# Two row maxima read by one VectorE instruction, in the attention steps without dense work

## The chip, the core and the metric

The kernel runs on one core of one Trainium2 chip. A core has five engines with queues of their own: TensorE (PE; its weight loads are shown as PEld), VectorE (DVE), ScalarE (ACT), GpSimd (POOL) and SyncE (SP, which issues the transfers here). Matmul results go to banks of 512 float32 values a partition, of which this kernel uses eight, and VectorE and ScalarE read them from there. The metric is device time in microseconds, lower is better.

## The reference

One block of a transformer with adaptive layer norm, over 2048 rows of 512, in float32: attention with 32 heads of 16, then a dense block with mish.

```python
h = _layernorm(x) * (1 + ca) + sa
q, k, v = ...                       # h @ wqkv, 32 heads of 16
scores = jnp.einsum("bhqd,bhkd->bhqk", q, k) * scale
p = _softmax(scores, axis=-1)
x = x + ga * (jnp.einsum("bhqk,bhkd->bhqd", p, v) ... @ wo)
h = _layernorm(x) * (1 + cb) + sb
x = x + gb * (mish(h @ w1 + b1) @ w2)
```

The six vectors `sa, ca, ga, sb, cb, gb` come from `silu(c) @ w_mod`. The softmax needs the largest score of each row (a query of a head) before the exponentials; that largest score is what the change is about.

## The kernel before

The attention is cut into 32 passes (`NIT`): four blocks of 512 queries by eight groups of four heads. A pass has 16 steps, one for each 128 keys' worth of work, so there are T = 512 steps, after 20 steps of lead-in (`PRO`). The order of all work is written out by hand: `step(t)` emits the instructions of step t, each engine takes its own in that order, and the framework adds the waits that the data need. `run_hooks` and `do_specials` put loads, splits and other small work at fixed half-steps.

Products of 64 rows are used throughout. The operands `ka` (keys) and `qa` (queries) hold two heads, one in partitions 0 to 63 and one in 64 to 127, with high and low parts of the numbers as extra rows. A matmul on one half of the rows can run beside one on the other half. A step t has three kinds of them:

- four **scores** (`score`, matmul L519): 128 keys by 512 queries, each followed at once by the exponential on ScalarE (L527) into `pr`. They are all on one half s of the rows; s changes from step to step.
- four **maxima** (`max_tile`, matmul L478): 128 queries by 512 keys (one key block `kb` of four), each followed by a reduction along the row on VectorE (L480), which writes one column of `mx`. They belong to the pass that comes 20 steps later (`tm = t + PRO`). For a query tile and a head the four key blocks give four columns, which `neg_max` (L489) and `max_rows` turn into the row's maximum, and two rows of `qa` later take it off the scores.
- **dense halves** (`mm_half`, L132): the projections, the output projection and the dense block, cut into units and dealt out over the steps by `next_part`. A unit's products run on the half of the rows that the scores leave free.

After these, `pv(t - 2)` issues the value products (L547) of the step two before: four matmuls of 32 columns that accumulate in the bank `acc`.

How the maxima are laid depends on f, the number of dense products of this step. `o = max(0, (8 - f) // 2)` maxima go to the free half (`alone`), the other 4 - o go to the scores' half (`mo`). With f = 0 all four are on the free half, and the last branch of the loop emits score, maximum, score, maximum. f is 0 where no unit is ready; the plan of units leaves that in steps 0, 1, 116 to 135 and 152 to 157. From step 492 on (`tm >= T`) there are no maxima.

Scores and maxima both write to the **ring**, six banks of one tile `ring_t`. `ring(w)` hands out the next bank, or the next two with `w = 2`, for which it first goes on to an even bank. With four scores and four maxima a step takes eight banks out of the six in turn, and the next step begins two further on. A matmul into a bank waits for the reader of what stood there before. After all is emitted, `free_banks` takes away waits between instructions that touch different banks of the ring; an instruction that reads two banks counts for both.

In `step`, `emit` runs a product and keeps what it returns (its exponential or reduction) where the next dense half has to wait for it (`cur["want"]`, `cur["after"]`).

Of the kernel before, what the change touches and what calls it, by code (L numbers as in the profile page):

```python
# [8 lines left out]
F32 = mybir.dt.float32  # L9
F32R = mybir.dt.float32r  # L10
AF = mybir.ActivationFunctionType
ALU = mybir.AluOpType
AX = mybir.AxisListType
# [5 lines left out]
def adaln_block(ctx: ExitStack, tc: tile.TileContext, x, wqkv, wo, w1, b1, w2, c, w_mod, out):  # L19
    nc = tc.nc  # L20
    P = 128
# [6 lines left out]
    TB = 512  # L28
# [4 lines left out]
    T = 16 * NIT  # L33
# [13 lines left out]
    x = x[0]  # L47
    out = out[0]
# [27 lines left out]
    for k in range(DK):  # L76
# [3 lines left out]
                            axis=AX.XY)  # L80
# [66 lines left out]
    def ring(w=1):  # L147
        if w == 2 and ring_at[0] % 2:
            ring_at[0] += 1
        b = ring_at[0] % NRING  # L150
        ring_at[0] += w
        return ring_t[:, b, :] if w == 1 else ring_t[:, b:b + 2, :]
# [37 lines left out]
    NR = 5  # L190
    kq = ctx.enter_context(tc.tile_pool(name="kq", bufs=1))
    ka = [kq.tile([P, S], F32R, name=f"ka{i}") for i in range(2)]
    qa = [kq.tile([P, TB], F32R, name=f"qa{i}") for i in range(NR)]
# [116 lines left out]
    with ExitStack() as es:  # L310
# [28 lines left out]
        e = lp.tile([P, DK], F32, name="sil_e")  # L339
# [46 lines left out]
        pr, pm = [], ring()[:, :2 * DK].rearrange("p (i k) -> p i k", k=DK)  # L386
        for i in range(2):
            pr.append(ring())
            for k in range(DK):
                nc.tensor.matmul(pr[i][32 * k:32 * k + 32, :], sil[:, k:k + 1].to_broadcast([P, 32]), wma[i][:, k, :],  # L390
                                 start=True, stop=True)
# [67 lines left out]
    ap = ctx.enter_context(tc.tile_pool(name="ap", bufs=1, reuse_waits="tile"))  # L459
# [8 lines left out]
    mxs = {}  # L468

    def max_tile(n, j, s, qs, kb):  # L470

        if n not in mxs:
            mxs[n] = ap.tile([P, 2, 8, 4], F32, tag="mx", name="mx", bufs=2)

        def product():
            kt, qt = ka[(2 * n + j) % NR], qa[(2 * n + j) % NR]
            pm = ring()
            nc.tensor.matmul(pm, qt[64 * s:64 * s + 64, qs * P:(qs + 1) * P], kt[64 * s:64 * s + 64, kb * TB:(kb + 1) * TB],  # L478
                             start=True, stop=True)
            return nc.vector.tensor_reduce(out=mxs[n][:, s, 4 * j + qs, kb:kb + 1], in_=pm, op=ALU.max, axis=AX.X)  # L480

        return product

    def neg_max(n):

        mx = mxs.pop(n)
        mm = ap.tile([P, 4, 2, 4], F32, tag="mm", name="mm", bufs=2)
        twice = bass.AP(tensor=mx.tensor, offset=mx.offset, ap=[list(mx.ap)[0], [16, 4], [0, 2], [4, 4], [1, 4]])
        nc.vector.tensor_reduce(out=mm, in_=twice, op=ALU.max, axis=AX.X)  # L489
        ats.setdefault(16 * n + 16 - PRO, []).append(lambda: max_rows(n, mm))  # L490
# [48 lines left out]
    def pv(t):  # L539
        if not 0 <= t < T:  # L540
            return
        n, kc = divmod(t, 16)
        if kc == 0:
            accs[n] = bank("acc")
        for h in range(4):
            o = (kc * 4 + h) * VW
            nc.tensor.matmul(accs[n][32 * h:32 * h + 32, :], vgs[n][:, o:o + 32], pts.pop((t, h)),  # L547
                             start=(kc == 0), stop=(kc == 15))
        if kc == 15:
            evac(n)  # L550
# [551 lines left out]
    cur = {"left": [], "fin": None, "part": [], "first": True}  # L1102
# [27 lines left out]
    def whole_units(h, credit):  # L1130

        while credit > 0:
            if not cur["left"]:
                if not units or h < units[0][0]():
                    return
                cur["tag"] = "acc" if cur.get("tag") == "ms" else "ms"
                cur["h"] = h
                cur["fin"] = units.pop(0)[1](cur["tag"])
                cur["left"] = list(pe_queue)
                pe_queue.clear()  # L1140
            m = cur["left"].pop(0)
            cur["first"] = False
            mm_go(m)
            credit -= m[0].shape[-1] / TB
            if not cur["left"]:
                at(h + 1, lambda fin=cur["fin"]: fin(h + 1))
                cur["fin"] = None

    def maxima(n, u, s, others):

        j, qs = divmod(u, 4)
        return ([max_tile(n, j, s, qs, kb) for kb in range(4 - others)],
                [max_tile(n, j, 1 - s, qs, kb) for kb in range(4 - others, 4)])

    def step(t):
        second = t % 2
        n, u = t // 16, t % 16 // 2
        tm = t + PRO
        run_hooks(2 * t)
        if t < 0:  # L1160

            for i in range(2):
                if tm < 16:
                    kb, jq = divmod(2 * tm + i, 8)
                else:
                    jq, kb = tm % 16 // 2, 2 * second + i
                for s in range(2):
                    max_tile(tm // 16, jq // 4, s, jq % 4, kb)()
            if second and tm % 16 == 15:
                neg_max(tm // 16)  # L1170
            run_hooks(2 * t + 1)
            for f in ats.pop(t, []):
                f()
            whole_units(2 * t + 1, CREDIT)
            do_specials(2 * t + 1)
            return
        s = 0 if second else 1
        own, others = ([score(n, j, v, 2 * u + i) for i in range(2) for j in range(2)] for v in (s, 1 - s))
        if not second and 1 < t < T:
            next_part(2 * t)  # L1180
        part = list(cur["part"])
        f = len(part)
        if t >= T:
            if t == T:
                cur["tag"] = "acc"
            run_hooks(2 * t + 1)
            pv(t - 2)
            whole_units(2 * t + 1, 8)
            do_specials(2 * t + 1)
            return  # L1190
        swap, held = False, None
        if tm < T:
            o = max(0, (8 - f) // 2)
            mo, alone = maxima(tm // 16, tm % 16 // 2, s, o)

            mine = [x for p in zip(mo, own) for x in p] + own[len(mo):]
            kinds = [k for p in zip("m" * len(mo), "s" * len(mo)) for k in p] + ["s"] * (len(own) - len(mo))
            swap = 2 <= f <= len(mine) and kinds[f - 1] == "s" and kinds[f - 2] == "m"
            if swap:
                mine[f - 2:f] = mine[f - 1], mine[f - 2]  # L1200
        else:
            o = max(0, (4 - f) // 2)
            mine = own[o:] if second else own[:4 - o]
            alone = others[4 - o:] if second else others[:o]

            m = len(mine)
            if f > m:
                mine = [mine[(i * m) // f] if (i + 1) * m // f > i * m // f else None for i in range(f)]
        beside = part + alone

        def emit(product):
            e = product()
            if cur.pop("want", None):
                cur["after"] = e

        ends = second and f and not cur["left"]
        for i in range(max(len(mine), len(beside))):
            if i == len(mine) // 2:
                run_hooks(2 * t + 1)
            if i < f:  # L1220
                last = i + 1 == f
                if i < len(mine) and mine[i] and not last:
                    if swap and ends and i + 2 == f:
                        held = mine[i](True)
                    else:
                        emit(mine[i])
                for m in beside[i]:
                    mm_half(m, second, cur["first"], bool(ends and last and m is beside[i][-1]),
                            cur.pop("after", None))
                    cur["first"] = False  # L1230
                if last:
                    if ends:
                        cur["fin"](2 * t + 2)
                        cur["fin"] = None
                    if held:
                        held()
                    cur["want"] = True
                    if i < len(mine) and mine[i]:
                        emit(mine[i])
            else:  # L1240
                for x in (*mine[i:i + 1], *beside[i:i + 1]):
                    emit(x)
        if tm < T and tm % 16 == 15:
            neg_max(tm // 16)
        do_specials(2 * t + 1, False)
        pv(t - 2)
        if t in ats:
            for f in ats.pop(t):
                f()
        else:  # L1250
            do_specials(2 * t + 1, True)

    def do_specials(h, behind=None):
        if specials and behind in (None, specials[0][2]) and h >= specials[0][0]():
            fin = specials.pop(0)[1]()
            pe_run()
            at(h + 1, lambda: fin(h + 1))
# [94 lines left out]
    def run_hooks(h):  # L1352
        while h in hooks:
            for f in hooks.pop(h):
                f()
# [37 lines left out]
```

## Time and profile before

| | us |
|---|---|
| median of 3 runs | 1679.77 |
| lowest and highest run | 1678.62, 1679.84 |
| the profiled execution | 1677.17 |
| its span in the profile | 1675.4 |
| VectorE busy in it | 1425.7 |
| ScalarE busy in it | 1336.4 |
| GpSimd busy in it | 910.9 |

The profile is one execution. Its page gives busy time by engine and groups of instructions by line; other views group instructions by line in a stretch of time, or list them in order of time. A group's line shows engine, operation, what is written from what, shape and count, then busy time and the mean length of one, then how long the engine sat idle before them and which instruction ended that. Matmul ends are modelled, so a busy TensorE isn't TensorE at its peak. A wait is put to the releaser that came last.

### The profile page before, as it was taken

What the parts mean: (1) busy time and instruction counts of PE and PEld (TensorE: products, weight loads), DVE (VectorE), ACT (ScalarE), POOL (GpSimd) and SP (SyncE); (2) the same over time, 40 slices, a digit from 0 to 9 for tenths busy, and PEclk for the clock granted to TensorE, in tenths of its full rate; (3) what the DMA queues carried; (4) which work ended last, traced back from release to release, by engine and by line L of the source; (5) the groups of instructions that cost most, each with busy time, mean ns of one, the idle gap of its engine ahead of it and who ended that gap; (6) DMA issues with size and microseconds to landing.
All of it is one profiled execution on the core that took longest, in us unless ns stands there. A gap on an engine that the chain in (4) does not pass through costs nothing.

```text
span 1675.4 us, 33101 instructions
## 1 busy us (share of the span) xinstructions
PE 1649.3 (98%) x12316; PEld 921.4 (55%) x12316; DVE 1425.7 (85%) x2327; ACT 1336.4 (80%) x2625; POOL 910.9 (54%) x938
## 2 busy tenths in 40 slices
PE   7999999999999999999999999999999999999999
PEld 5755665555435455555555555555555555554687
DVE  6888898888998988888888888888888888882577
ACT  6257778787779899888889898888889889889364
POOL 5155215465434398854535498654535597645532
PEclk9999999999999999999999999999999999999999
DMA  7677456777684443435343644334442645332362
GB/s 253 186 224 226 110 168 198 236 229 226 201 254 113 111 107 86 119 78 160 86 126 75 200 105 97 102 108 121 121 102 72 178 104 134 87 116 84 126 228 73
DMA packets 113992, 240.03 MB, mean 143 GB/s; under 512 B 24048, under 2 KB 49648, under 8 KB 107784
## 3 DMA queue, kind: packets, MB, share of 16 engines
q1 hardware_dynamic: 113832, 237.92, 50.4%
q8 instruction: 97, 1.59, 0.4%
q14 instruction: 63, 0.52, 0.1%
HBM read 179.95 MB, written 51.44 MB: 138 GB/s over the span
## 4 chain that ended last, share of the span: by engine, by line
PE 83%; POOL 5%; DMA 4%; ACT 4%; DVE 2%; SPq 1%; issue 1%; ACTq 0%; DVEq 0%; POOLq 0%
PE bk L547 27%; PE ring L478 22%; PE ring L519 21%; PE bk L132 6%; PE ring L126 2%; ACT pr L527 2%; PE ring L1088 2%; DMA ka<-kscr 1%; PE bk L126 1%; DVE mx L480 1%; DMA wr<-in_A_wqkv 1%; DMA xt<-in_A_x 1%; POOL rr L781 1%; POOL ee L779 1%; POOL hb L786 1%
## 5 line engine op out<-in xcount | busy, mean ns | idle before, releaser
L480 DVE TENSOR_REDUCE mx<-ring 128x1 f32<-128x512 f32 x2048 | 1278.8, 684 | 159.5 <-PE bk L132 96.0
L527 ACT ACTIVATE pr<-ring 128x512 f32<-128x512 f32 x2048 | 1087.8, 603 | 197.9 <-PE bk L132 159.8
L478 PE MATMUL ring<-ka,qa 64*128 64x512 f32 x2048 | 773.9, 425 | 1.5 <-ACT pr L527 0.8
L519 PE MATMUL ring<-qa,ka 64*128 64x512 f32 x2048 | 719.3, 395 | 6.6 <-ACT pr L527 4.9
L478 PEld LDWEIGHTS ring<-ka,qa 64*128 64x128 f32 x2048 | 365.9, 184 | 396.0 <-DVE mx L480 351.6
L547 PE MATMUL bk<-pr,vg 128*32 128x512 f32 x4096 | 545.1, 604 | 0.0
L519 PEld LDWEIGHTS ring<-qa,ka 64*128 64x128 f32 x2048 | 374.3, 184 | 113.8 <-ACT pr L527 37.7
L132 PE MATMUL bk<-h,w 64*128 64x512 f32 x1008 | 279.9, 409 | 0.0
L132 PE MATMUL bk<-w,a_h 64*128 64x512 f32 x576 | 194.7, 417 | 1.2 <-ACT pr L527 0.6
L132 PEld LDWEIGHTS bk<-h,w 64*128 64x128 f32 x1008 | 171.5, 184 | 2.9 <-ACT yd L906 0.9
L547 PEld LDWEIGHTS bk<-pr,vg 128*32 128x32 f32 x4096 | 80.9, 108 | 127.2 <-issue 120.0
L132 PE MATMUL bk<-w,a_l 64*128 64x512 f32 x288 | 113.9, 396 | 0.0
L749 POOL TENSOR_SCALAR ee<-hb 128x512 f32<-128x512 f32 x42 | 62.5, 1488 | 93.6 <-ACT hb L743 85.1
L132 PEld LDWEIGHTS bk<-w,a_h 64*128 64x128 f32 x576 | 95.4, 185 | 5.3 <-ACT pr L527 1.8
L779 POOL TENSOR_TENSOR ee<-ee,rr 128x512 f32<-128x512 f32 x42 | 54.0, 1285 | 75.5 <-ACT rr L770 75.3
L132 PE MATMUL bk<-w,o_hl 64*128 64x512 f32 x288 | 79.5, 408 | 0.0
L98 POOL TENSOR_TENSOR a_l<-hb,a_h 128x512 fp32r<-128x512 f32 x53 | 71.7, 1354 | 4.4
L907 POOL TENSOR_TENSOR y<-yd,y 128x512 f32<-128x512 f32 x40 | 51.5, 1287 | 28.2 <-ACT yd L906 28.0
L502 POOL TENSOR_TENSOR mt<-mt,mh 32x128 fp32r<-32x128 f32 x32 | 14.4, 450 | 87.9 <-ACT mh L501 87.9
L132 PE MATMUL bk<-h_h,wl 64*128 64x512 f32 x168 | 56.8, 418 | 0.0
L787 POOL TENSOR_TENSOR hb<-hb,rr 128x512 f32<-128x512 f32 x42 | 54.5, 1298 | 3.3
L764 POOL TENSOR_TENSOR ee<-ee,rr 128x512 f32<-128x512 f32 x42 | 54.0, 1287 | 3.5
(211 smaller groups left out, 1847.9 us busy)
## 6 DMA issues: line engine op xcount, KB each, us to landing
ka<-kscr SPq DMA_DIRECT2D x124, 384.0 KB
w<-w2scr SPq DMA_DIRECT2D x56, 512.0 KB
w<-w1scr SPq DMA_DIRECT2D x46, 512.0 KB
vg<-vscr SPq DMA_DIRECT2D x32, 552.0 KB
qa<-qscr SPq DMA_DIRECT2D x124, 100.0 KB
kscr<-qh SPq DMA_DIRECT2D x16, 512.0 KB
qscr<-qh SPq DMA_DIRECT2D x32, 256.0 KB
w1scr<-hl SPq DMA_DIRECT2D x14, 512.0 KB
```

What stands on the lines that cost most here:

```text
L98: (nc.gpsimd if eng == "p" else nc.vector).tensor_sub(lo, src, hi.bitcast(F32))
L132: i = nc.tensor.matmul(acc, l[64 * g:64 * g + 64], r[64 * g:64 * g + 64], start=start, stop=stop)
L478: nc.tensor.matmul(pm, qt[64 * s:64 * s + 64, qs * P:(qs + 1) * P], kt[64 * s:64 * s + 64, kb * TB:(kb + 1) * TB], start=True, stop=True)
L480: return nc.vector.tensor_reduce(out=mxs[n][:, s, 4 * j + qs, kb:kb + 1], in_=pm, op=ALU.max, axis=AX.X)
L519: nc.tensor.matmul(p_, kt[64 * s:64 * s + 64, kc * P:(kc + 1) * P], qt[64 * s:64 * s + 64, :], start=True, stop=True)
L527: e = nc.scalar.activation(pr, p_, AF.Exp, scale=SCALE)
L547: nc.tensor.matmul(accs[n][32 * h:32 * h + 32, :], vgs[n][:, o:o + 32], pts.pop((t, h)), start=(kc == 0), stop=(kc == 15))
L749: nc.gpsimd.tensor_scalar_min(buf("ee", 2), b["hb"], HCAP)
L764: nc.gpsimd.tensor_mul(ee, ee, rr)
L779: nc.gpsimd.tensor_mul(ee, ee, rr)
L787: nc.gpsimd.tensor_mul(hb, hb, rr)
L907: nc.gpsimd.tensor_add(y[i], yd, y[i])
```

## The change

In a step with f = 0 and maxima to make, the four maxima come from the new `max_pairs`. The product for an even key block takes two neighbouring banks of the ring and writes the first; it has no reduction and returns nothing. The product for the next key block writes the second bank, and one reduction reads both banks (128 x 2 x 512) and writes two neighbouring columns of `mx`. Such a step emits maximum, score, maximum, score, in place of score first. Since a product may now return nothing, `emit` asks for that. Steps with dense halves, and those from 492 on, are as before.

```diff
+    def max_pairs(n, u, s):
+
+        if n not in mxs:
+            mxs[n] = ap.tile([P, 2, 8, 4], F32, tag="mx", name="mx", bufs=2)
+        j, qs = divmod(u, 4)
+        made = []
+
+        def product(kb):
+            kt, qt = ka[(2 * n + j) % NR], qa[(2 * n + j) % NR]
+            if kb % 2 == 0:
+                made.append(ring(2))
+            pm = made[-1]
+            nc.tensor.matmul(pm[:, kb % 2, :], qt[64 * s:64 * s + 64, qs * P:(qs + 1) * P],
+                             kt[64 * s:64 * s + 64, kb * TB:(kb + 1) * TB], start=True, stop=True)
+            if kb % 2:
+                return nc.vector.tensor_reduce(out=mxs[n][:, s, 4 * j + qs, kb - 1:kb + 1], in_=pm, op=ALU.max, axis=AX.X)
+
+        return [lambda kb=kb: product(kb) for kb in range(4)]
...
-            mo, alone = maxima(tm // 16, tm % 16 // 2, s, o)
+            mo, alone = maxima(tm // 16, tm % 16 // 2, s, o) if f else ([], max_pairs(tm // 16, tm % 16 // 2, 1 - s))
...
-            if cur.pop("want", None):
+            if e is not None and cur.pop("want", None):
                 cur["after"] = e
...
-                for x in (*mine[i:i + 1], *beside[i:i + 1]):
+                for x in (*mine[i:i + 1], *beside[i:i + 1]) if f or tm >= T else (beside[i], mine[i]):
                     emit(x)
```

## The prediction

> **What bounds the kernel now.** I read the page first, for the engine shares and for the group of reductions that the change joins.
>
> ```profile
> span 1675.4 us, 33101 instructions
> PE 1649.3 (98%) x12316; PEld 921.4 (55%) x12316; DVE 1425.7 (85%) x2327; ACT 1336.4 (80%) x2625; POOL 910.9 (54%) x938
> ...
> L480 DVE TENSOR_REDUCE mx<-ring 128x1 f32<-128x512 f32 x2048 | 1278.8, 684 | 159.5 <-PE bk L132 96.0
> ```
>
> TensorE is nearly always occupied, so time added to its queue anywhere shows in the end. The change touches only steps whose dense part is empty. To find them I asked for busy time by stretch, of the dense halves' line L132 alone; the columns are the stretch, its length, busy time and count on PE and on PEld, granted clock, DMA share and GB/s.
>
> ```profile
> 102.50:106.50 4.00, 0.00 (x0) 0.00 (x0) 1.00 0.65 188
> ...
> 438.79:493.91 55.12, 0.00 (x0) 0.00 (x0) 1.00 0.80 228
> 493.91:539.95 46.04, 26.49 (x96) 16.43 (x96) 1.00 0.47 132
> 539.95:557.04 17.09, 0.00 (x0) 0.00 (x0) 1.00 0.47 165
> ```
>
> The same view for the reductions L480, busy time and count on DVE:
>
> ```profile
> 438.79:493.91 55.12, 49.56 (x80) 1.00 0.80 228
> 539.95:557.04 17.09, 14.78 (x24) 1.00 0.47 165
> ```
>
> Four reductions make a step, so these stretches are 20 and 6 steps without dense halves (steps 116 to 135 and 152 to 157 by the plan of units); the first row is steps 0 and 1. That is 28 of 512 steps, some 76 us: 17.09 + 55.12 + 4.00. The timeline shows one of them (start, duration, engine, line; weight loads mostly left out).
>
> ```profile
> 449.73 1.07 PE L547 MATMUL bk<-pr,vg 128*32 128x512 f32 x8
> 450.72 0.49 PE L519 MATMUL ring<-qa,ka 64*128 64x512 f32 x1
> ...
> 450.73 0.49 PE L478 MATMUL ring<-ka,qa 64*128 64x512 f32 x1
> ...
> 451.06 0.39 PE L519 MATMUL ring<-qa,ka 64*128 64x512 f32 x1
> ...
> 451.06 0.39 PE L478 MATMUL ring<-ka,qa 64*128 64x512 f32 x1
> ...
> 451.25 1.57 ACT L527 ACTIVATE pr<-ring 128x512 f32<-128x512 f32 x3 [0.66 <-PE ring L478]
> 451.29 1.88 DVE L480 TENSOR_REDUCE mx<-ring 128x1 f32<-128x512 f32 x3 [0.24 <-PE ring L478]
> 451.29 0.39 PE L519 MATMUL ring<-qa,ka 64*128 64x512 f32 x1
> 451.29 0.39 PE L478 MATMUL ring<-ka,qa 64*128 64x512 f32 x1
> ...
> 451.90 0.18 PEld L519 LDWEIGHTS ring<-qa,ka 64*128 64x128 f32 x1 [0.62 <-ACT pr L527]
> ...
> 452.03 0.50 PE L478 MATMUL ring<-ka,qa 64*128 64x512 f32 x1
> ...
> 452.46 0.64 PE L547 MATMUL bk<-pr,vg 128*32 128x512 f32 x4
> ```
>
> The step repeats every 2.73 us (449.73 to 452.46). Its pairs of score (L519) and maximum (L478), one on each half of the array's rows, start at 450.72, 451.06 and 451.29. The fourth stops for 0.61 us. The ring has six banks and a pair takes two, so the fourth pair takes the banks of the first: its score waits for the first exponential (from 451.25) and its maximum for the first reduction (451.29 + 0.684 = 451.97, matmul at 452.03, so 0.06 from the end of a read to the release). So the limit here is a delay round the ring, not VectorE's load: value products, first pair, its readers, fourth pair. Waits in the 20 steps say the same: waiter, releaser, us, times, longest.
>
> ```profile
> PEld ring L519 <- ACT pr L527: 27.8, 39, 1.1
> ```
>
> **The change part by part.** Two single reductions become one over two banks. For its length, from the groups of VectorE by form (busy, mean ns):
>
> ```profile
> L562 DVE COPY ot<-bk 128x256 f32<-128x256 f32 x32 | 13.6, 424 | 6.9 <-PE bk L547 6.9
> ...
> L906 DVE COPY yd<-bk 128x512 f32<-128x512 f32 x1 | 0.7, 690 | 8.8 <-PE ring L519 8.8
> ```
>
> 256 more elements from the matmul banks cost 690 - 424 = 266 ns, so 512 more cost 0.53 us and the joint read takes 0.684 + 0.53 = 1.22 us. No row shows a reduction of 1024. Bounds: 1.07 if there were no fixed part (1024 elements at 1.04 ns), 1.37 for two whole reads. I take 1.22, the slope of the nearest rows. What joining saves in VectorE's pace is less than 1.37 - 1.22, for single reads overlap already:
>
> ```profile
> 103.41 7.26 DVE L480 TENSOR_REDUCE mx<-ring 128x1 f32<-128x512 f32 x12 [0.85 <-PE ring L478]
> ```
>
> Twelve end to end give (7.26 - 0.684) / 11 = 0.60 each, so a pair goes from 1.20 to about 1.13 and a step saves 0.13 us of VectorE. The Trainium skill (VectorE: DVE Perf Modes, section "The DRAIN you can't avoid") has the next operation start only when the pipe of the one before is empty; by that rule a step would save 2 x 0.15 = 0.30 us. The trace's 0.60 us spacing against 0.684 us of one speaks against it.
>
> What moves is the release of banks. Call a step's banks r0 to r5 in the order of taking. Now the first pair of maxima takes r0 and r1, its scores r2 and r3, the second pair of maxima r4 and r5, and the last two scores come round to r0 and r1. The third score so waits for the joint read of the **same step**, which can start only when the second maximum is made. And since a step takes eight banks of six, the next step begins two further on: its first two scores land on this step's r4 and r5 and wait for the second joint read. The order max, score, max, score is one queue, so the fourth maximum stands behind the third score, and the next step's second maximum behind its first score. Both joint reads are in a loop with TensorE.
>
> The lags come from rows. Behind a released matmul, the other half's follows in 0.03 us; the last matmul of a step starts 0.32 us ahead of the value products when it isn't held:
>
> ```profile
> 105.95 0.50 PE L478 MATMUL ring<-ka,qa 64*128 64x512 f32 x1
> ...
> 105.98 0.50 PE L519 MATMUL ring<-qa,ka 64*128 64x512 f32 x1
> ```
>
> ```profile
> 1525.28 1.06 PE L547 MATMUL bk<-pr,vg 128*32 128x512 f32 x8
> ...
> 1527.08 0.39 PE L519 MATMUL ring<-qa,ka 64*128 64x512 f32 x1
> 1527.40 0.64 PE L547 MATMUL bk<-pr,vg 128*32 128x512 f32 x4
> ```
>
> A read starts 0.56 us after a first matmul (450.73 to 451.29, 0.07 after its end), and by the same 0.07 it starts 0.39 + 0.07 = 0.46 after one in a run. Let the third score start at 0. The fourth starts at 0.34 (450.72 to 451.06), the value products at 0.66, and the next step's first pair 0.99 later at 1.65. The fourth maximum started at 0.03, so the second joint read runs from 0.59 to 1.81, and the next step's first score goes at 1.87. Its second maximum can start at 1.99 (0.34 behind the first), its read at 2.45 to 2.55, ends at 3.67 to 3.77, and the third score goes at 3.73 to 3.83. I take **3.80** (the held score breaks the run, so the longer lag is nearer). A step loses 3.80 - 2.73 = 1.07 us; 26 steps lose **27.8 us**.
>
> Steps 0 and 1 have no value products ahead of them, and are paced by the twelve reductions above.
>
> ```profile
> 102.87 0.50 PE L478 MATMUL ring<-ka,qa 64*128 64x512 f32 x1
> ...
> 109.60 1.06 PE L547 MATMUL bk<-pr,vg 128*32 128x512 f32 x8
> ```
>
> With joint reads the four run one after the other: second maximum at 103.21, read 103.67 to 104.89, held score 104.95, next read 105.55 to 106.77, then 107.43 to 108.65 and 109.31 to 110.53. Step 2's third slot needs a bank of that last read: 110.59, then 0.34 and four times 0.23 to its last slot at 111.85, and value products at 112.2 in place of 109.60: **+2.5 us**, between +1.5 (step 3 starts with VectorE less behind) and +4.
>
> No DMA, hook or queue of SP or POOL moves against the steps: eight banks are taken per step as before, so later bank numbers stand too. The exponentials of the last two scores come 1 us later, but their readers come two steps on. The sum is 30.3 us. The profiled run took 1677.17 us (span 1675.4, 1.8 around it), so 1707.5 by its own time; the median shown, 1679.77, is 2.6 above that run, so **1710**.
>
> **The rivals.** *Not slower: VectorE's saving counts.* It decides if the third score doesn't wait longer than the fourth pair does now, that is, if r0 is free by 1.18 us after the first pair (450.72 to 451.90). The joint read ends at 0.34 + 0.46 + 1.22 = 2.02, 0.8 too late; it would need the first bank to be given back half way through the read. Nothing in the trace shows such a release; every bank wait ends after its reader. If it were so, the step would go toward VectorE's 2 x 1.13 + 0.24 = 2.5 us, 0.23 under now: 28 steps, -6 us, 1673. The floor is the 2.12 us of a step without maxima (1525.28 to 1527.40).
>
> *Given back.* The added time would let late transfers land and shorten later waits. But the 16 dense steps between the stretches already take 46.04 / 16 = 2.88 us on a busy TensorE, so there is nothing near 27 us to recover: 1680.
>
> *The clock falls.* TensorE would pause some 1.4 us in every step. It has paused about as long here, with no loss of clock (columns: PE, PEld, DVE, ACT, POOL busy, then the granted clock):
>
> ```profile
> 102.84 0.18 PEld L519 LDWEIGHTS ring<-qa,ka 64*128 64x128 f32 x1 [1.38 <-DVE mx L480]
> ```
> ```profile
> 100.50:104.50 4.00, 2.82 (x14) 1.65 (x13) 3.15 (x6) 2.33 (x5) 3.73 (x5) 1.00 0.72 255
> ```
>
> At half the clock TensorE's part of the loop (0.34 + 0.32 + 0.99 + 0.34 + 0.46 = 2.45 us) would come twice: 26 x 2.45 = 64 us more, 1774. The Trainium skill (TensorE: Matmul & The Clock Gate, "A second HAM failure mode: psum-queue depth-cycling") tells of a kernel in which cycling through banks made TensorE pause so often that its clock went to and fro. By that page the time would go towards this rival's; the clock of 1.00 above speaks against it, for single pauses.
>
> *Does the change do what it says?* A joint read split into two would show 2048 reductions of 512 still; the access is plain, two neighbouring banks, so I count it within the range's upper bound.
>
> **How the numbers follow.** Forecast, slower by some 30 us: 0.90. Not slower by the early release: 0.05 (0.04 faster, 0.01 same). Given back: 0.02. The clock: 0.03. With a read of 1.07 us a step takes 3.65 and the sum is 26 x 0.92 + 2 = 26 us, 1706; with 1.37, both reads count (0.59 + 1.37 + 0.06 + 0.03, then 0.56 + 1.37 + 0.06 = 4.04) and the sum is 26 x 1.31 + 3 = 37, 1717. With 1 to 2 us for the lags, 1704 to 1718; cases outside hold about 0.15. 0.2% (3.4 us) is about what a measurement of this kernel can tell from no change. Faster 0.04, same 0.03, slower 0.93.
>
> **What would show it.** 56 reductions over 128x1024, near 1.22 us; the 20-step stretch at about 76 us in place of 55.12, with a wait of scores (L519) for the reduction in place of that for the exponential, twice a step; dense steps unchanged. A step still at 2.73 or less would refute the ring's turn; a step much beyond 4.04 would point to the clock or to a wait that I don't see.

## The result and the profile after

| | before | changed |
|---|---|---|
| median, us | 1679.78 | 1706.78 |
| lowest and highest of 4 runs | 1678.62, 1679.84 | 1706.01, 1708.73 |
| profiled execution, us | 1677.17 | 1708.73 |
| its span | 1675.4 | 1707.0 |

The changed kernel is slower by a factor of 1.0161, 95% interval 1.0149 to 1.0173, or 27.0 us between the medians. The forecast was 1710, with 1704 to 1718 as its range.

From the page of the changed kernel, the span and the engines' busy time:

```profile
span 1707.0 us, 33044 instructions
PE 1657.6 (97%) x12316; PEld 924.2 (54%) x12316; DVE 1425.8 (84%) x2271; ACT 1338.9 (78%) x2625; POOL 909.6 (53%) x938
```

VectorE has 56 instructions fewer and is busy for as long as before (1425.8 against 1425.7): joining the reads gave it nothing back. Its groups by form show why:

```profile
L480 DVE TENSOR_REDUCE mx<-ring 128x1 f32<-128x512 f32 x1936 | 1209.8, 685 | 152.5 <-PE bk L132 93.6 <-PE ring L478 56.7
L499 DVE TENSOR_REDUCE mx<-ring 128x2 f32<-128x1024 f32 x56 | 68.6, 1225 | 36.3 <-PE ring L496 31.0 <-PE ring L538 5.3
```

A joint read is 1.225 us long. But single reads overlap, and joint ones here never do: each has idle time of VectorE ahead of it, 36.3 us in all. (In this kernel the lines are 19 further down: scores are L538, the exponential L546, the value products L566; the maxima of the changed steps are L496, their joint read L499.)

Busy time by stretch, of the joint reads alone. The columns are the stretch, its length, busy time and count on DVE, granted clock, DMA share and GB/s. The stretches run from the first value products of one step to those of another: the 20 steps, the 16 dense ones behind them, the 6 steps. (The joint read counted in the dense stretch is the last of the 20 steps; it runs over.)

```profile
445.48:519.74 74.26, 47.86 (x40) 1.00 0.64 189
519.74:565.87 46.13, 1.13 (x1) 1.00 0.37 99
565.87:588.97 23.10, 13.49 (x12) 1.00 0.35 121
```

The 20 steps take 74.26 us in place of 55.12, the six 23.10 in place of 17.09, and the dense ones between them 46.13, as before (46.04). That is 19.1 + 6.0 = 25.1 us. One step, from the timeline:

```profile
455.93 0.50 PE L538 MATMUL ring<-qa,ka 64*128 64x512 f32 x1 [1.08 <-DVE mx L499]
...
455.93 0.49 PE L496 MATMUL ring<-ka,qa 64*128 64x512 f32 x1
...
456.27 0.39 PE L538 MATMUL ring<-qa,ka 64*128 64x512 f32 x1
...
456.50 1.22 DVE L499 TENSOR_REDUCE mx<-ring 128x2 f32<-128x1024 f32 x1 [0.62 <-PE ring L538]
...
456.59 1.06 PE L566 MATMUL bk<-pr,vg 128*32 128x512 f32 x8
...
457.59 0.50 PE L496 MATMUL ring<-ka,qa 64*128 64x512 f32 x1
...
457.78 0.50 PE L538 MATMUL ring<-qa,ka 64*128 64x512 f32 x1
...
457.93 0.39 PE L496 MATMUL ring<-ka,qa 64*128 64x512 f32 x1
...
458.35 1.23 DVE L499 TENSOR_REDUCE mx<-ring 128x2 f32<-128x1024 f32 x1 [0.47 <-PE ring L496]
...
459.63 0.49 PE L538 MATMUL ring<-qa,ka 64*128 64x512 f32 x1 [1.08 <-DVE mx L499]
```

Read it from the third score at 455.93: fourth maximum beside it, joint read from 456.50, next step's first score released at 457.78, second maximum at 457.93, joint read from 458.35 to 459.58, third score at 459.63. The loop is 3.70 us. Before, the fourth score waited for an exponential; the waits of the 20 steps now name the joint read, once on the weight load and once on the matmul:

```profile
PEld ring L538 <- DVE mx L499: 29.8, 20, 1.6
...
PE ring L538 <- DVE mx L499: 21.4, 20, 1.1
```

The two spans differ by 31.6 us: 25.1 in the 26 steps, 3.4 from the first score to the first value products (102.87 to 109.60 before, 105.97 to 116.11 now), and 3.1 ahead of that, where the kernels are alike. Kernels that leave the beginning as it was also had the first score there: at 106.19, 105.23 and 105.58 us in the traces of e4, e5 and e8 below. So the 3.1 us belong to the single execution.

### The profile page after: what moved, and what is told of

Same layout as the page of the kernel before. It is cut to its first block, busy times and chain, and to the rows that moved or that the text cites. A ratio compares the mean times of both kernels' runs of the same rounds, so it can differ in the third digit from the quotient of the medians.

```text
span 1707.0 us, 33044 instructions
## 1 busy us (share of the span) xinstructions
PE 1657.6 (97%) x12316; PEld 924.2 (54%) x12316; DVE 1425.8 (84%) x2271; ACT 1338.9 (78%) x2625; POOL 909.6 (53%) x938
## 4 chain that ended last, share of the span: by engine, by line
PE 86%; DVE 4%; POOL 4%; DMA 3%; ACT 2%; issue 1%; SPq 1%; ACTq 0%; POOLq 0%; DVEq 0%
PE bk L566 27%; PE ring L478 21%; PE ring L538 21%; PE bk L132 7%; PE ring L126 3%; DVE mx L499 2%; PE bk L126 2%; PE ring L1107 2%; DMA qscr<-ql 1%; ACT pr L546 1%; PE ring L496 1%; DMA wr<-in_A_wqkv 1%; DMA ka<-kscr 1%; DMA wma<-in_w_mod 1%; POOL hb L806 0%
## 5 line engine op out<-in xcount | busy, mean ns | idle before, releaser
L480 DVE TENSOR_REDUCE mx<-ring 128x1 f32<-128x512 f32 x1936 | 1209.8, 685 | 152.5 <-PE bk L132 93.6
L546 ACT ACTIVATE pr<-ring 128x512 f32<-128x512 f32 x2048 | 1090.0, 603 | 224.1 <-PE bk L132 147.0
L538 PE MATMUL ring<-qa,ka 64*128 64x512 f32 x2048 | 718.6, 395 | 30.6 <-DVE mx L499 29.7
L478 PE MATMUL ring<-ka,qa 64*128 64x512 f32 x1936 | 732.3, 424 | 0.9 <-ACT pr L546 0.3
L478 PEld LDWEIGHTS ring<-ka,qa 64*128 64x128 f32 x1936 | 347.6, 184 | 395.1 <-DVE mx L480 350.9
L566 PE MATMUL bk<-pr,vg 128*32 128x512 f32 x4096 | 545.1, 604 | 0.0
L538 PEld LDWEIGHTS ring<-qa,ka 64*128 64x128 f32 x2048 | 373.0, 185 | 116.0 <-DVE mx L499 42.1
L566 PEld LDWEIGHTS bk<-pr,vg 128*32 128x32 f32 x4096 | 80.9, 108 | 130.4 <-issue 123.2
L499 DVE TENSOR_REDUCE mx<-ring 128x2 f32<-128x1024 f32 x56 | 68.6, 1225 | 36.3 <-PE ring L496 31.0
L798 POOL TENSOR_TENSOR ee<-ee,rr 128x512 f32<-128x512 f32 x42 | 53.9, 1284 | 75.5 <-ACT rr L789 75.3
```

Source lines behind the costliest of these rows:

```text
L538: nc.tensor.matmul(p_, kt[64 * s:64 * s + 64, kc * P:(kc + 1) * P], qt[64 * s:64 * s + 64, :], start=True, stop=True)
L546: e = nc.scalar.activation(pr, p_, AF.Exp, scale=SCALE)
L798: nc.gpsimd.tensor_mul(ee, ee, rr)
```

## Experiments

Theory A: the time comes from when banks are given back. A joint read holds two banks until its end, and in a ring of six, of which a step takes eight, the third score and the next step's first score stand behind such reads. Rival B: a read over two banks is itself slow. Rival C: the order, maximum ahead of score, does it. Times of the 20 and 6 steps below are taken, as above, between starts of value products in each trace.

**e1: banks and order of the change, single reads.**

```diff
-            if kb % 2:
-                return nc.vector.tensor_reduce(out=mxs[n][:, s, 4 * j + qs, kb - 1:kb + 1], in_=pm, ...)
+            return nc.vector.tensor_reduce(out=mxs[n][:, s, 4 * j + qs, kb:kb + 1], in_=pm[:, kb % 2, :], ...)
```

> Banks and order of the changed kernel, but each bank read by a reduction of its own. Theory A (release of banks: the third score waits for the reader of its own step's first maximum): the score waits only to the end of the first single read, 0.57 + 0.68 + 0.06 = 1.31 us after the first pair, and the fourth to the end of the second, about 1.91; value products at 2.34, next pair at 3.33, so a step of about 3.3 us between 2.73 and 3.70, and some 1694 to 1697 us in all. Rival B (the read over two banks is what costs, the turn of the banks is harmless): 2.73 us a step, 1680. Rival C (the length of the read doesn't matter at all, only the order): 3.70 us a step, 1707.

Measured: 1694.72 us, ratio 1.0083 (1.0068 to 1.0099). A step from the timeline (L537 score, L496 maximum, L498 single read, L565 value products):

```profile
458.03 1.07 PE L565 MATMUL bk<-pr,vg 128*32 128x512 f32 x8
...
459.02 0.49 PE L496 MATMUL ring<-ka,qa 64*128 64x512 f32 x1
...
460.30 0.50 PE L537 MATMUL ring<-qa,ka 64*128 64x512 f32 x1 [0.31 <-DVE mx L498]
...
460.90 0.50 PE L537 MATMUL ring<-qa,ka 64*128 64x512 f32 x1
...
461.33 1.06 PE L565 MATMUL bk<-pr,vg 128*32 128x512 f32 x8
```

The third score goes 1.28 us after the first pair (459.02 to 460.30; 1.31 was said), the fourth at 1.88, and a step takes 3.30 us. So the change's 0.97 us a step has two parts: 0.57 because both last scores follow the step's own first two maxima in turn, and 0.40 that come with the joint reads, which give both banks back only at their end. B and C both fall as whole explanations. That the 0.40 are the late release, and not a read that is slow in itself, only e3 and e8 below show.

**e2: the order alone.** The kernel before, with the change's last hunk (maximum, then score) and nothing else.

> The kernel before with maximum ahead of score in the steps without dense halves, nothing else. Theory A: no wait changes its place, since a pair still takes two banks and comes round to the same kinds three pairs later; 2.73 us a step, 1680 (1678 to 1682). Rival C (the order by itself holds the score back): over 3 us a step, 1688 or more.

Measured: 1679.28 us, ratio 0.9993 (0.9984 to 1.0003); the 20 steps take 55.46 us. The order costs nothing. One part of the expectation was wrong: a wait does change its place. The maximum is now first in the queue, so the wait in the ring is now put to the reduction and no longer to the exponential (the weight loads of the 20 steps, 40 times), and a step in the middle takes 2.70 us.

```profile
PEld ring L478 <- DVE mx L480: 29.4, 40, 0.8
```

**e3: joint reads, but no product behind one of its own step.** Two banks for the scores, two for each pair of maxima; the order is score, max, score, max, max, max, score, score.

```diff
+        if not f and tm < T:
+            ring_at[0] += -ring_at[0] % NRING
...
+            two = ring(2)
+            for i, x in enumerate((mine[0], beside[0], mine[1], *beside[1:], mine[2], mine[3])):
...
+                if x in mine:
+                    x(p_=two[:, mine.index(x) % 2, :])
+                else:
+                    x()
```

> Joint reads kept, but the scores of such a step have two banks of their own and each pair of maxima two; order score, max, score, max, max, max, score, score. Theory A: no product waits for a joint read of its own step; the third score waits for the first exponential (1.18 us after the first pair), the fourth for the second (1.70), value products at about 2.1, so 3.05 to 3.1 us a step, 9 us over the kernel before: 1687 to 1691. Rival B (joint reads of 1.22 us are themselves too slow or collide with the matmuls): a step stays near 3.7 us, 1704 to 1707.

Measured: 1693.45 us, ratio 1.0073 (1.0058 to 1.0088).

```profile
456.09 1.07 PE L566 MATMUL bk<-pr,vg 128*32 128x512 f32 x8
...
457.08 0.50 PE L538 MATMUL ring<-qa,ka 64*128 64x512 f32 x1
...
457.88 2.36 DVE L499 TENSOR_REDUCE mx<-ring 128x2 f32<-128x1024 f32 x2 [0.74 <-PE ring L496]
458.26 0.18 PEld L538 LDWEIGHTS ring<-qa,ka 64*128 64x128 f32 x1 [0.42 <-ACT pr L546]
...
458.75 0.18 PEld L538 LDWEIGHTS ring<-qa,ka 64*128 64x128 f32 x1 [0.30 <-ACT pr L546]
...
459.18 0.16 PEld L566 LDWEIGHTS bk<-pr,vg 128*32 128x32 f32 x8 [0.24 <-issue]
```

A step takes 3.09 us, as A says: the same 1.22 us reads, now two end to end in 2.36 us, and the last scores wait for exponentials. The whole is 2.5 us over the expected range. The trace's six steps took 21.27 us where 6 x 3.09 is 18.5: small transposes take banks of the ring there, and the fixed layout runs into them; and from the first score to the first value products it took 8.89 us against 6.73 before, most of it at a clock of 0.50 (granted from 105.5 to 112.3 us).

**e4: the kernel before, value products ahead of the fourth pair.**

```diff
+                if i == 3 and not f and tm < T:
+                    pv(t - 2)
                 for x in (*mine[i:i + 1], *beside[i:i + 1]):
...
+        if f or tm >= T:
+            pv(t - 2)
```

> The kernel before, with the value products of these steps issued between the third and the fourth pair. If the step of 2.73 us is a delay round the ring (the fourth pair waits for the readers of the first while TensorE stands still), the value products fill that wait and the step falls to VectorE's pace of four reductions at 0.60, 2.40 us: some 8 us less, 1670 to 1673. Rival (VectorE or ScalarE sets 2.73 us already): 1679 to 1681.

Measured: 1681.39 us, ratio 1.0000 (0.9990 to 1.0009). The expectation fails:

```profile
453.71 1.07 PE L547 MATMUL bk<-pr,vg 128*32 128x512 f32 x8
...
454.70 0.50 PE L519 MATMUL ring<-qa,ka 64*128 64x512 f32 x1
...
455.89 0.50 PE L519 MATMUL ring<-qa,ka 64*128 64x512 f32 x1 [0.21 <-ACT pr L527]
...
456.44 1.06 PE L547 MATMUL bk<-pr,vg 128*32 128x512 f32 x8
```

The step is still 2.73 us. The fourth pair goes at once at 454.70, but between two groups of value products there are four pairs wherever one puts them, and the ring holds three. The fourth behind the value products now is the next step's third, and it starts 1.19 us behind the first (1.18 before). I had taken away one wait and not looked which pair would stand there next.

**e5: joint reads from step 116 on only** (`if f or t < 2` in both conditions).

> The changed kernel, but with single reductions in steps 0 and 1 as before. In the trace of the changed kernel the way from the first score to the first value products took 10.14 us against 6.73, and the granted clock fell to 0.50 in it. Theory A with the clock: that goes, so about 3.4 us under the changed kernel, 1703 to 1704, and the clock stays at 1.00 throughout. Rival (the clock fell by chance, or the price sits in the 26 steps alone): 1706 to 1707.

Measured: 1706.43 us, ratio 1.0154 (1.0139 to 1.0169). The first score to the first value products took 6.93 us in its trace, and the 20 steps 74.24. But the whole was expected at 1703 to 1704, and the clock at 1.00 throughout; both failed. The clock fell there too (0.62 granted between 108 and 112 us), so its fall isn't bound to joint reads. Against the changed kernel's 1706.78 the whole can't tell 3.4 us from nothing, which e9 does.

**e6: the change, value products ahead of the third score.**

```diff
+                    if i == 2 and not f and tm < T and x is mine[i]:
+                        pv(t - 2)
                     emit(x)
...
+        if f or tm >= T:
+            pv(t - 2)
```

> The changed kernel with the value products issued ahead of the third score, into the time in which it waits. Theory A with two loops: the loop through the second joint read (score at 0, fourth maximum, read from 0.57 to 1.79, next step's first score 1.85, second maximum, read from 2.4, third score about 3.65 to 3.70) holds the step alone, so nothing is won: 3.65 to 3.70 us a step, 1705 to 1708. Rival (only the third score's wait counts and TensorE's 0.99 us of value products stands in the way behind it): about 2.7 us a step, 1681.

Measured: 1708.62 us, ratio 1.0172 (1.0158 to 1.0185), 0.6 us over the expected range.

```profile
463.70 1.07 PE L566 MATMUL bk<-pr,vg 128*32 128x512 f32 x8
...
466.73 0.50 PE L538 MATMUL ring<-qa,ka 64*128 64x512 f32 x1 [0.88 <-DVE mx L499]
...
467.39 1.06 PE L566 MATMUL bk<-pr,vg 128*32 128x512 f32 x8
```

3.69 us: nothing won. The value products now lie in the third score's wait, and the next step's first score still waits for the second joint read (second row). The loop through these holds the step without the value products.

**e7 and e10: the kernel before with a seventh bank.** The bank `ms`, which the dense units leave free in the 26 steps, takes the fourth maximum, ahead of the fourth score.

```diff
+                if i == 3 and not f and 2 <= t < T - PRO:
+                    beside[3](bank("ms"))
+                    emit(mine[3])
+                    ring_at[0] += 1
+                    continue
```

> The kernel before, but in the 26 steps without dense halves the fourth maximum goes, ahead of the fourth score, to the bank that the dense units leave free there. Theory A (the step is a delay round the banks): the fourth score still waits for the first exponential, 1.18 us after the first pair, but the fourth maximum no longer for the first reduction (1.31), so 0.13 us a step less: 2.60 us, 3 us less in all, 1677 to 1679 beside a kernel before at 1680 to 1681. Rival (value products or VectorE's pace): 2.73 us and no difference.

> The kernel of the seventh bank once more, for one question: in its trace step 128 stood 3.27 us for the rows of the maxima that SyncE copies into qa, and the clock fell to 0.50 behind it. If that wait comes from the shorter steps, it is there again and the 20 steps take about 58 us; if it was a late transfer of that one execution, the 20 steps take about 52.5 us (20 x 2.61 and 0.3 for the rest) at a clock of 1.00.

Measured: e7 1679.59 us, ratio 1.0003 (0.9994 to 1.0012), which can't be told from the kernel before and lies just above the expected 1677 to 1679; e10, the same kernel, 1679.03 in its one run. In e10's trace the step is what was said, 2.60 us:

```profile
457.72 1.06 PE L547 MATMUL bk<-pr,vg 128*32 128x512 f32 x8
...
459.52 0.39 PE L478 MATMUL bk<-ka,qa 64*128 64x512 f32 x1
...
459.90 0.50 PE L519 MATMUL ring<-qa,ka 64*128 64x512 f32 x1
...
460.32 1.07 PE L547 MATMUL bk<-pr,vg 128*32 128x512 f32 x8
```

Its 20 steps took 52.96 us at a clock of 1.00 (55.12 before), the six 16.76 (17.09), the dense ones between 46.49 (46.04): some 2 us in all, under what was expected and within the noise. e7's own trace had 58.61 us for the 20 steps, for one wait, which e10 doesn't have; so it isn't the shorter steps that make it:

```profile
479.05 0.47 PE L519 MATMUL ring<-qa,ka 64*128 64x512 f32 x1 [3.27 <-DMA qa<-mt]
```

**e8: joint reads on seven banks.** Steps 0 and 1 as before; in the 26 steps scores go to two banks of the ring and to `ms`, and only the fourth score waits, for the first exponential.

```diff
+            two = ring(2)
+            to = [two[:, 0, :], two[:, 1, :], bank("ms"), two[:, 0, :]]
+            for i in range(4):
...
+                if i == 3:
+                    beside[3]()
+                mine[i](p_=to[i])
+                if i < 3:
+                    beside[i]()
```

> Joint reads in the 26 steps, each on two banks of its own; scores on two banks of the ring and on the bank that the dense units leave free, so that only the fourth score waits, for the first exponential. Steps 0 and 1 as before. Theory A: joint reads cost nothing where no product waits for one, 2.60 us a step, 1676 to 1680, at or a little under the kernel before. Rival B (a joint read is slow in itself): 3 us a step or more, 1688 and over.

Measured: 1683.07 us, ratio 1.0017 (1.0008 to 1.0026), 3 us above the upper end of what A said and 5 below what B said.

```profile
462.78 1.07 PE L566 MATMUL bk<-pr,vg 128*32 128x512 f32 x8
...
465.43 1.06 PE L566 MATMUL bk<-pr,vg 128*32 128x512 f32 x8
...
557.03 0.49 PE L538 MATMUL ring<-qa,ka 64*128 64x512 f32 x1 [0.68 <-ACT hf L880]
```

A step with joint reads takes 2.65 us, less than the 2.73 of the kernel before, and the 20 steps 54.59. The six took 19.91: the first score stands behind the reader of a transpose that took the same bank (third row). So a joint read costs little where no product waits for it (0.05 us a step beside the 2.60 of e10, with seven banks and single reads), and the layout gives its gain back elsewhere.

**e9: joint reads in steps 0 and 1 alone.**

> Joint reads in steps 0 and 1 alone; the other 26 steps as before. In two traces with joint reads there, the way from the first score to the first value products took 10.14 and 10.47 us, in six with single reads 6.2 to 6.9, so the trace should again show some 10.2 us with the clock falling to 0.50. If that is on the path that sets the end (theory A), the whole is 3 to 3.5 us longer than the kernel before, 1683 to 1684 beside 1680 to 1681. Rival (given back): the steps behind them stand on the load of w_mod anyway, which then ends sooner as seen from there, and the whole differs by under 1 us.

Measured: 1683.45 us, ratio 1.0020 (1.0011 to 1.0030), 1.8 to 5.0 us. First score to first value products: 10.45 us. The time is on the path. In these two executions 0.5 of the 3.7 us are won back by the value products of step 14, which come 36.12 us behind the first in place of 36.59.

## Why the prediction was right

- **The steps.** 28 steps, and 56 joint reads of 1.225 us (1.22 was said, from the slope of two copies).
- **The ring's turn.** Third score behind the joint read of its own step, next step's first score behind the second: both waits stand in the trace where they were put. e1 parts them from the read's length, e3 and e8 take them away with the reads kept, e6 shows that the loop through the second read holds the step without the value products.
- **The size of a step.** 3.80 was taken, 3.70 measured. Of the lags, the fourth score at 0.34, value products at 0.66, first pair at 1.66 (1.65 said), first score at 1.85 (1.87) and second maximum at 2.00 (1.99) hold. The term that was mis-sized is the start of its read: 0.42 us after it (457.93 to 458.35), where the prediction took the longer end of 0.46 to 0.56 with "the held score breaks the run, so the longer lag is nearer". The run wasn't broken for the maximum: its matmul lasted 0.39 us, and even the shorter end was 0.04 too long.
- **The sum.** 27.0 us were measured against 30.3. 26 steps cost 25.1 us against 27.8. Steps 0 and 1 cost 3.4 in the trace and 1.8 to 5.0 by e9 against 2.5. That this is near is in part luck, for two errors go against each other. The first held score came 1.82 us behind the first score (105.97 to 107.79) where 2.08 was said: the first maximum had gone ahead, at 104.67, while the first score waited for a transfer. And the clock was not thought of: at 1.00 the first two joint reads start 1.85 us apart (106.51 and 108.36), at 0.50 the next ones 2.14.

```profile
110.50 1.22 DVE L499 TENSOR_REDUCE mx<-ring 128x2 f32<-128x1024 f32 x1 [0.92 <-PE ring L496]
...
112.64 1.22 DVE L499 TENSOR_REDUCE mx<-ring 128x2 f32<-128x1024 f32 x1 [0.92 <-PE ring L496]
```

- **The rivals.** No bank was given back early, so nothing was faster. Nothing near 25 us was recovered: the dense steps stand at 46.13. The clock did not fall in the 26 steps (1.00 in both stretches above), but it did in steps 0 to 2, so that rival had a part of the truth. With the lags of the prediction these steps would have taken 9.3 us (102.87 to 112.2), and 9.1 with the first held score where it was; three traces (the changed kernel, e9, e6) show 10.14, 10.45 and 10.47, so 1.1 to 1.4 us is an estimate of the clock's share. The row with which the prediction argued against this rival, a pause of 1.38 us, is that of the weight loads: the matmuls of the kernel before stood 0.99 us there, and 1.08 a step in the changed kernel.
- **VectorE's pace.** The 0.13 us that joining saves a step holds: in e3 two joint reads take 2.36 us, so 1.135 from one to the next, where 1.13 was said. But the prediction held the spacing of single reads, 0.60 us, against the rule that it cites there. The same section of the Trainium skill (VectorE: DVE Perf Modes, "The DRAIN you can't avoid") says that a next operation that is not held starts earlier. So the spacing does not speak against that section.

## What to carry to other kernels

In these kernels a product waits for the whole instruction that read its bank, so a read over two banks gives both back at its end (the read to 459.58, the released score at 459.63). In a short ring, write down which later product takes each bank and count the loop from release to release before counting the instructions saved. Where single reads already overlap (0.60 us apart here at 0.68 us each), joining two saves a twentieth of their time (1.20 us against 1.135), not a fixed cost each. And a wait that is filled by moving other work comes back one turn of the ring later if the ring is what is short (e4); another bank shortened the step (2.60 us against 2.73, e10), though the whole kernel not measurably.

## What the runs showed of the hardware that was not expected

The clock fell where the prediction didn't expect it, and the busy time of TensorE in the profile does not tell when. In the rows above TensorE was busy for 1.50 of 3.40 us in pieces, and the clock then stood at 0.50 from 108.4 to 115.3 us; at 2.62 of 3.40 it stayed at 1.00 through 20 steps, each with a pause of more than a microsecond. In e7 the 3.27 us wait for a transfer was followed by the same:

```profile
476.80:480.20 3.40, 1.15 (x7) 0.75 (x7) 0.61 (x2) 0.65 (x2) 0.00 (x0) 0.95 0.86 299
480.20:483.60 3.40, 3.40 (x14) 1.20 (x15) 1.87 (x4) 1.43 (x3) 0.00 (x0) 0.50 1.03 224
```

That looks like a limit on the busy share, but two other traces do not fit one. In e3 the clock fell behind a stretch with TensorE busy for 2.98 of 3.42 us (first two rows); in e4 it stayed at 1.00 in and behind one with 2.04 of 3.41 (last two):

```profile
102.09:105.51 3.42, 2.98 (x12) 1.44 (x12) 2.38 (x3) 2.49 (x5) 2.23 (x3) 1.00 0.74 227
105.51:112.33 6.82, 6.51 (x30) 3.52 (x28) 5.13 (x6) 4.15 (x8) 0.00 (x0) 0.50 0.87 267
...
104.41:107.82 3.41, 2.04 (x11) 1.04 (x9) 2.18 (x4) 2.33 (x5) 3.24 (x5) 1.00 0.68 224
107.82:111.23 3.41, 3.34 (x18) 1.85 (x18) 3.41 (x7) 3.14 (x7) 1.27 (x1) 1.00 0.77 238
```

What makes it fall stays open. Around steps 0 to 2 it fell in eight of the twelve traces: in all four with joint reads there (the changed kernel, e3, e6, e9), for 6.8 us, and in four of the eight with single reads (e2, e5, e7, e10), for 3.4 us. So joint reads are not needed for the fall. In e6 it fell once more inside the six steps, for 3.4 us from 585.0 us.

The Trainium skill (TensorE: Matmul & The Clock Gate, "What's actually happening") puts the fall to half clock behind an idle window of about 3.4 us. The length fits these traces: but for the end of each kernel, the times at 0.50 are 3.4 or 6.8 us. That TensorE must be idle in the window does not fit, since it was busy for 1.50 and 2.98 us in stretches of about that length ahead of a fall.
